# Block-sorted attention into a routed expert layer: values regrouped through DRAM, output turned by DMA transposes, and half-chunk first-layer blocks

## The chip, the cores and the metric

The kernel runs on one core of one Trainium2 chip. The metric is the device time of one execution in microseconds (us). Before the change it is 749.72 us, the median of 3 runs (749.62 to 749.95).

## The reference

Two stages follow each other. The first is an attention whose keys and values are sorted by blocks; the second a layer of eight experts that mixes all experts for each token.

```python
# q, k, v: batch 4, heads 8, seq 768, head_dim 64; sort_net: 4 x 8 x 8 x 8
P = sort_net
for _ in range(5):                       # Sinkhorn
    P = exp(P - max(P, -1)); P /= sum(P, -1); P /= sum(P, -2)
k_sorted = einsum('bhij,bhjcd->bhicd', P, k_blocks)     # 8 blocks of 96 rows
v_sorted = einsum('bhij,bhjcd->bhicd', P, v_blocks)
attn = softmax(q_block @ k_sorted_block.T / 8)          # within each block of 96
out  = attn @ v_sorted_block

x = out as 3072 tokens x 512             # (batch, seq) x (head, dim)
P = exp(x @ w_gate - max)                # 3072 x 8, then 8 Sinkhorn rounds
y = sum over e of P[:, e] * (relu(x @ w1[e]) @ w2[e])   # w1: 512x1024, w2: 1024x512
```

## The kernel before, in words

Matrix products are in bf16 with float32 sums. The attention works on 16 **pairs** of heads (pair m is heads 2m and 2m+1; four pairs make one batch). A token's row of 768 is split as 128 partitions x 6 (`p kk`), so that a block of 96 rows is 16 partitions x 6. `load_pair` (L83) loads k, v and q of one pair, 192 KB each in SBUF, with a cast from float32, from GpSimd's queue.

**Start.** `sort_net` is loaded, TensorE runs 24 filler matmuls on zeros (L116), and VectorE and ScalarE run the 5 Sinkhorn rounds (L121 to L135). `Prep` holds P widened to 1024 columns; eight matmuls (L140) make `Pbig`, from which `build_r` (L154) makes R of each pair, a 128x128 matrix per head that sorts blocks when it is multiplied.

**One pair passes through four stages**, each one iteration of the loop over m later than the one ahead of it:

- `stage1(m)` (L162): 12 matmuls for K and 12 for V (L171) give the sorted K and V with the head dimension on partitions, evicted as `KT` and `VT` (L176, L178); 12 transposes by TensorE (L182) and one copy (L185) give `QT`; then `build_r(m + 1)`.
- `stage2(m)` (L189): 16 matmuls for the scores (L197), four Exps (L200); 8 transposes by TensorE (L204) and a copy (L207) give `VS`, the sorted V with rows on partitions and a column of ones for the sum.
- `stage3(m)` (L209): 16 matmuls with V (L216), then four times a reciprocal and a scaling (L219, L220) into `OG`.
- `stage4(m)` (L223): 8 transposes by TensorE (L227) and one copy (L229) into `xtT`, the input of the second layer with features on partitions.

**Blocks between the stages.** Each iteration calls `fill(1)` four times (L268). It issues the next first-layer block `h_block` (L244): four matmuls of 512 columns (L249) for one expert e, one chunk c of 512 tokens and 128 of the 1024 hidden features, evicted with a ReLU by VectorE or ScalarE in turn (L253, L255). A chunk is free only when `state["done"]` has reached its last batch (`last_batch`); the list `early` gives the order. As long as no batch is done, `fill` issues one filler matmul (L266) in place of a block. `gate(b)` (L232) computes the logits of a batch. After the loop come 8 Sinkhorn rounds with three blocks in each (L312), and then the main part: second-layer tiles `y_tile` (L335: eight matmuls, L339, and one eviction with an add, L345) alternate with the remaining blocks. `HB` = 10 buffers hold first-layer chunks. The last expert's tiles are stored by SP (L349).

All engines run in the order in which the code issues (`tc.manual_schedule`). PSUM's eight banks are a pool that rotates. SP's queue has only the load of `sort_net` and the 24 stores; GpSimd's queue has all other loads (w1 at L95, w2 at L99). Tokens in `xtT` lie as `kk p`, so the stores at L349 write rows six apart.

Of the kernel before, what the change touches and what calls it, by code (L numbers as in the profile page):

```python
# [25 lines left out]
def kernel(  # L26
# [17 lines left out]
    HB = 10  # L44
    scale = 1.0 / (D ** 0.5)
# [6 lines left out]
    ps = ctx.enter_context(tc.tile_pool(name="ps", bufs=8, space=bass.MemoryType.PSUM))  # L52

    def bank(shape, dt=F32):
        return ps.tile(shape, dt, name="bank")
# [8 lines left out]

# [6 lines left out]
    mask = ones.tile([128, 16], F32)  # L71
    nc.vector.reduce_sum(out=mask, in_=ident.rearrange("p (j c) -> p c j", c=16), axis=AX.X)
# [6 lines left out]
    iop = actx.enter_context(tc.tile_pool(name="iop", bufs=5))  # L79
    atp_ = actx.enter_context(tc.tile_pool(name="atp", bufs=2))  # L80
    qkv = {}

    def load_pair(m):  # L83
        r = []
        for src, nm in ((kh, "kb"), (vh, "vb"), (qh, "qb")):
            t = iop.tile([128, 2, 6, 64], BF16, name=nm)
            nc.gpsimd.dma_start(out=t, in_=src[2 * m:2 * m + 2].rearrange("h p kk d -> p h kk d"))  # L87
            r.append(t)
        qkv[m] = r
# [11 lines left out]
    for m in range(4):  # L101
        load_pair(m)
# [3 lines left out]
    xtT = ones.tile([128, 4, B, 6, 128], BF16)  # L106
    xf = xtT.rearrange("d hp b kk p -> d hp (b kk p)")
# [6 lines left out]
    w_ = bank([128, 512])  # L114
    for _ in range(24):
        nc.tensor.matmul(w_, wide[:, 0:128], wide, start=True, stop=True)  # L116

    rs = ones.tile([32, 8], F32)
    Prep = ones.tile([32, 8, 8, 16], BF16)
    Pt = P.rearrange("p i j -> p j i")  # L120
    nc.vector.reduce_max(out=rs, in_=P, axis=AX.X)  # L121
    nc.vector.tensor_sub(P, P, mkap(rs, [rs.ap[0], rs.ap[1], [0, 8]]))
    for it in range(5):
        nc.scalar.activation(out=P, in_=P, func=AF.Exp)
        nc.vector.reduce_sum(out=rs, in_=P, axis=AX.X)
        nc.vector.reciprocal(out=rs, in_=rs)
        nc.vector.tensor_tensor(out=P, in0=P, in1=mkap(rs, [rs.ap[0], rs.ap[1], [0, 8]]),
                                op=ALU.mult)
        nc.vector.reduce_sum(out=rs, in_=Pt, axis=AX.X)
        nc.vector.reciprocal(out=rs, in_=rs)  # L130
        if it < 4:
            nc.vector.tensor_tensor(out=Pt, in0=Pt, in1=mkap(rs, [rs.ap[0], rs.ap[1], [0, 8]]),
                                    op=ALU.mult)
        else:
            nc.vector.tensor_tensor(out=Prep, in0=mkap(P, [P.ap[0], [8, 8], [1, 8], [0, 16]]),  # L135
                                    in1=mkap(rs, [rs.ap[0], [0, 8], [1, 8], [0, 16]]), op=ALU.mult)

    pbp = bank([128, 8, 32])
    for i in range(8):
        nc.tensor.matmul(pbp[:, i, :], Prep[:, i].rearrange("g j c -> g (j c)"),  # L140
                         ident[0:32, 0:32], start=True, stop=True)
    Pbig = ones.tile([128, 8, 32], F32)
    nc.vector.tensor_copy(Pbig, pbp)


    KT, VT, QT, ATT, VS, OG = {}, {}, {}, {}, {}, {}

    vs_ = [ones.tile([96, 8, 2, 65], BF16, name=f"vs{n}") for n in range(2)]
    for t in vs_:
        nc.vector.memset(t[:, :, :, 64:65], 1.0)  # L150

    Rt = {}

    def build_r(m):  # L154
        R = Rt[m] = atp_.tile([128, 2, 8, 16], BF16, name="R")
        nc.vector.tensor_tensor(
            out=R,
            in0=mkap(Pbig, [Pbig.ap[0], [1, 2], [32, 8], [0, 16]], off=2 * m),
            in1=mkap(mask, [mask.ap[0], [0, 2], [0, 8], [1, 16]]),
            op=ALU.mult)  # L160

    def stage1(m):  # L162
        kb, vb, qb = qkv[m]
        R = Rt[m]
        for src, dic, nm in ((kb, KT, "KT"), (vb, VT, "VT")):
            dic[m] = atp_.tile([128, 8, 6, 16], BF16, name=nm)
            for kh2 in range(2):
                b_ = bank([128, 3, 128])
                for k3 in range(3):
                    for h2 in range(2):  # L170
                        nc.tensor.matmul(b_[64 * h2:64 * h2 + 64, k3, :], src[:, h2, 3 * kh2 + k3, :],  # L171
                                         R[:, h2].rearrange("p i c -> p (i c)"), start=True, stop=True)
                dst = dic[m][:, :, 3 * kh2:3 * kh2 + 3, :].rearrange("d i kk c -> d kk i c")
                b_ = b_.rearrange("d kk (i c) -> d kk i c", c=16)
                if nm == "KT" or kh2 == 0:
                    nc.scalar.copy(dst, b_)  # L176
                else:
                    nc.vector.tensor_copy(dst, b_)  # L178
        b_ = bank([128, 6, 128], BF16)
        for kk in range(6):  # L180
            for h2 in range(2):
                nc.tensor.matmul(b_[64 * h2:64 * h2 + 64, kk, :], qb[:, h2, kk, :], ident,  # L182
                                 is_transpose=True, start=True, stop=True)
        QT[m] = atp_.tile([128, 6, 128], BF16, name="QT")
        nc.vector.tensor_copy(QT[m], b_)  # L185
        if m + 1 < NPAIR:
            build_r(m + 1)

    def stage2(m):  # L189
        ATT[m] = [atp_.tile([96, 2, 384], BF16, name=f"at{h2}") for h2 in range(2)]  # L190
        for half in range(2):
            bb = [bank([96, 4, 96]) for _ in range(2)]
            for i4 in range(4):
                i = half * 4 + i4
                for h2 in range(2):
                    hs = slice(64 * h2, 64 * h2 + 64)
                    nc.tensor.matmul(bb[h2][:, i4, :], KT[m][hs, i].rearrange("d kk c -> d (kk c)"),  # L197
                                     QT[m][hs, :, 16 * i:16 * i + 16], start=True, stop=True)
            for h2 in range(2):
                nc.scalar.activation(out=ATT[m][h2][:, half, :], in_=bb[h2].rearrange("k i q -> k (i q)"),  # L200
                                     func=AF.Exp, scale=scale)
        b_ = bank([96, 8, 128], BF16)
        for i in range(8):
            nc.tensor.matmul(b_[:, i, :], VT[m][:, i].rearrange("d kk c -> d (kk c)"), ident, is_transpose=True,  # L204
                             start=True, stop=True)
        VS[m] = vs_[m % 2]
        nc.vector.tensor_copy(VS[m][:, :, :, 0:64], b_.rearrange("c i (h d) -> c i h d", d=64))  # L207

    def stage3(m):  # L209
        OG[m] = atp_.tile([96, 8, 2, 64], BF16, name="OG")  # L210
        for half in range(2):
            for h2 in range(2):
                b_ = bank([96, 4, 65])
                for i4 in range(4):
                    i = half * 4 + i4
                    nc.tensor.matmul(b_[:, i4, :], ATT[m][h2][:, half, 96 * i4:96 * i4 + 96],  # L216
                                     VS[m][:, i, h2, :], start=True, stop=True)
                rc = atp_.tile([96, 4], F32, name="rc")
                nc.vector.reciprocal(out=rc, in_=b_[:, :, 64:65].rearrange("q i a -> q (i a)"))  # L219
                nc.vector.tensor_tensor(out=OG[m][:, 4 * half:4 * half + 4, h2, :], in0=b_[:, :, 0:64],  # L220
                                        in1=mkap(rc, [rc.ap[0], [1, 4], [0, 64]]), op=ALU.mult)

    def stage4(m):  # L223
        b, hpi = m // 4, m % 4
        b_ = bank([128, 8, 96], BF16)
        for i in range(8):
            nc.tensor.matmul(b_[:, i, :], OG[m][:, i].rearrange("q h d -> q (h d)"), ident[0:96, 0:96],  # L227
                             is_transpose=True, start=True, stop=True)
        nc.scalar.copy(xtT[:, hpi, b].rearrange("d kk (i c) -> d i kk c", c=16),  # L229
                       b_.rearrange("d i (kk c) -> d i kk c", c=16))  # L230

    def gate(b):  # L232
        b_ = bank([128, 6, E])
        for t in range(6):
            for kk in range(4):
                nc.tensor.matmul(b_[:, t, :], xtT[:, kk, b, t, :], wg[:, kk], start=(kk == 0),  # L236
                                 stop=(kk == 3))
# [3 lines left out]
    hT = {}  # L241
    flip = [0]

    def h_block(e, c, fb, both=False):  # L244
        if fb == 0:
            hT[e, c] = hp_.tile([128, 8, 512], BF16, name="hTs")
        b_ = bank([128, 512])
        for kk in range(4):
            nc.tensor.matmul(b_, w1t[e][:, kk, fb * 128:(fb + 1) * 128], xf[:, kk, c * 512:(c + 1) * 512],  # L249
                             start=(kk == 0), stop=(kk == 3))  # L250
        flip[0] ^= 1
        if both and flip[0]:
            nc.vector.tensor_scalar_max(hT[e, c][:, fb, :], b_, 0.0)  # L253
        else:
            nc.scalar.activation(out=hT[e, c][:, fb, :], in_=b_, func=AF.Relu)  # L255

    early = [(0, 0), (1, 0), (0, 1), (0, 2), (1, 1), (1, 2), (0, 3), (1, 3), (0, 4), (0, 5), (1, 4), (1, 5)]
    seq = early + [(e, c) for e in range(2, E) for c in range(6)]
# [147 lines left out]
```

The softmax here doesn't subtract the row's maximum and nothing guards it: scores larger than these inputs give would overflow.

## Time and profile before

| | us |
|---|---|
| median of 3 runs | 749.72 |
| the profiled execution | 750.19 |
| its span, first to last instruction | 748.4 |
| TensorE busy (matmuls / weight loads beside them) | 738.3 / 358.5 |
| ScalarE / VectorE / GpSimd busy | 274.2 / 252.1 / 48.9 |
| first-layer matmuls, L249 (1536) | 346.1 |
| second-layer matmuls, L339 (1536) | 338.0 |
| first sort (L171) starts at | 14.45 |
| iteration 7 starts at | 43.56 |
| first second-layer matmul at | 146.82 |

Times of day are us from the start of the span. "Busy" sums the instructions of an engine, with overlaps counted once. Matmuls are pipelined, so that the duration of one in the profile (379 ns for 512 columns) is more than its share of a row of them: in the chain of waits four take 0.86 us. The chain follows back from the last instruction, at each step to whatever ended the wait. The granted clock is the share of full speed that TensorE's throttle allowed. A DMA share over 1 means that transfers overlap within the engines.

### The profile page before, as it was taken

The page shows a single profiled execution, that of the slowest core. Times are in us where ns is not written, and L with a number is a line of the kernel's source. Part 1 is how long each engine was busy: PE and PEld are TensorE (multiplying, and loading weights), DVE is VectorE, ACT ScalarE, POOL GpSimd, SP SyncE. Part 2 cuts the span into 40 slices and gives each one's busy share as a digit, 9 for nine tenths or more (in the row PEclk, how much of TensorE's full clock was granted, in tenths as well). Part 3 has the DMA queues.
Part 4 walks back from the last instruction along what each step waited for, and adds up shares of the span by engine and source line. Part 5 has one row for each costly group of instructions (what it writes and reads, how often), then busy time and mean ns, then how long its engine had stood idle before and what let it go on. Part 6 is the DMA issues. An engine that isn't in the chain of part 4 may idle for free.

```text
span 748.4 us, 10663 instructions
## 1 busy us (share of the span) xinstructions
PE 738.3 (99%) x4588; PEld 358.5 (48%) x4588; DVE 252.1 (34%) x497; ACT 274.2 (37%) x497; POOL 48.9 (7%) x71
## 2 busy tenths in 40 slices
PE   6999999999999999999999999999999999999997
PEld 3776665444444444444444444444444444444443
DVE  5887775632122122122221221221221221212443
ACT  2776665513423423324324324234234233243000
POOL 8542000000000000000000000000000000000000
PEclk8999999999999999999999999999999999999999
DMA  9999100011300061200330032100330003000133
GB/s 149 204 205 163 19 2 1 1 20 38 56 1 1 0 96 29 46 1 1 56 57 1 0 57 40 19 0 1 57 56 1 1 0 57 1 0 1 43 154 141
DMA packets 29679, 33.21 MB, mean 44 GB/s; under 512 B 1984, under 2 KB 22464, under 8 KB 29632
## 3 DMA queue, kind: packets, MB, share of 16 engines
q0 software_dynamic: 26128, 26.23, 22.5%
q1 hardware_dynamic: 3504, 6.30, 2.2%
q8 instruction: 36, 0.59, 0.3%
q14 instruction: 11, 0.09, 0.0%
HBM read 52.45 MB, written 6.29 MB: 78 GB/s over the span
## 4 chain that ended last, share of the span: by engine, by line
PE 98%; DMA 1%; POOL 1%; DVE 0%; issue 0%; POOLq 0%
PE bank L249 44%; PE bank L339 44%; PE bank L171 2%; PE bank L216 2%; PE bank L204 1%; PE bank L197 1%; PE bank L266 1%; DMA qb<-in_q_dram 1%; PE bank L182 1%; PE bank L227 1%; PE bank L236 0%; POOL kb L87 0%; POOL vb L87 0%; PE bank L321 0%; POOL qb L87 0%; DVE osbl L345 0%
## 5 line engine op out<-in xcount | busy, mean ns | idle before, releaser
L255 ACT ACTIVATE hTs<-bank 128x512 bf16<-128x512 f32 x358 | 213.7, 597 | 371.2 <-PE bank L249 370.4
L249 PE MATMUL bank<-xtT,w1e 128*128 128x512 bf16 x1536 | 346.1, 379 | 0.0
L339 PE MATMUL bank<-w2e,hTs 128*128 128x512 bf16 x1536 | 338.0, 379 | 0.0
L345 DVE SCALAR_TENSOR_TENSOR osbl<-bank,glog,osbl 128x512 f32<-128x512 f32 x168 | 126.2, 751 | 398.7 <-PE bank L339 398.7
L339 PEld LDWEIGHTS <-hTs 128*128 128x128 bf16 x1536 | 150.2, 98 | 181.0
L249 PEld LDWEIGHTS <-w1e 128*128 128x128 bf16 x1536 | 147.9, 98 | 170.3
L342 DVE TENSOR_SCALAR osbl<-bank,glog 128x512 f32<-128x512 f32 x24 | 18.0, 751 | 54.7 <-PE bank L339 54.7
L220 DVE TENSOR_TENSOR OG<-bank,rc 96x256 bf16<-96x256 f32 x64 | 26.9, 421 | 2.2
L95 POOL DMA_DIRECT2D w1e<-in_moe_w_dram x8 | 6.0, 752 | 312.6 <-PE bank L249 312.3
L99 POOL DMA_DIRECT2D w2e<-in_moe_w_dram x8 | 7.1, 888 | 237.5 <-PE bank L339 237.1
L253 DVE TENSOR_SCALAR hTs<-bank 128x512 bf16<-128x512 f32 x26 | 17.7, 683 | 6.1 <-PE bank L249 6.1
L229 ACT COPY xtT<-bank 128x768 bf16<-128x768 bf16 x16 | 12.8, 798 | 14.1 <-PE bank L227 13.7
L176 ACT CAST KT<-bank 128x384 bf16<-128x384 f32 x32 | 13.8, 486 | 8.1 <-PE bank L171 7.9
L87 POOL DMA_DIRECT2D kb<-in_k_dram x16 | 11.5, 722 | 20.9 <-PE bank L171 20.1
L178 DVE CAST VT<-bank 128x384 bf16<-128x384 f32 x16 | 8.9, 553 | 11.2 <-PE bank L171 8.8
L219 DVE RECIPROCAL rc<-bank 96x4 f32<-96x4 f32 x64 | 10.9, 171 | 3.7 <-PE bank L216 3.7
L87 POOL DMA_DIRECT2D vb<-in_v_dram x16 | 11.5, 722 | 5.2 <-PE bank L266 2.5
L87 POOL DMA_DIRECT2D qb<-in_q_dram x16 | 11.6, 724 | 1.9 <-issue 0.3
L266 PE MATMUL bank<-wide 128*128 128x512 bf16 x28 | 10.6, 419 | 0.0
L204 PE MATMUL bank<-ident,VT 128*96 128x128 bf16 x128 | 10.4, 224 | 0.0
L171 PE MATMUL bank<-R,kb 128*64 128x128 bf16 x192 | 9.1, 234 | 1.0 <-DMA qb<-in_q_dram 1.0
L197 PEld LDWEIGHTS <-KT 64*96 64x96 bf16 x256 | 7.1, 121 | 5.8 <-issue 5.6
(152 smaller groups left out, 232.6 us busy)
## 6 DMA issues: line engine op xcount, KB each, us to landing
w1e<-in_moe_w_dram POOLq DMA_DIRECT2D x8, 1024.0 KB, 8.1
w2e<-in_moe_w_dram POOLq DMA_DIRECT2D x8, 1024.0 KB, 8.9
out_dram<-osbl SPq DMA_DIRECT2D x24, 256.0 KB, 2.0
kb<-in_k_dram POOLq DMA_DIRECT2D x16, 192.0 KB, 7.3
vb<-in_v_dram POOLq DMA_DIRECT2D x16, 192.0 KB, 7.3
qb<-in_q_dram POOLq DMA_DIRECT2D x16, 192.0 KB, 7.3
P<-in_sort_net_dram SPq DMA_DIRECT2D x1, 8.0 KB, 1.7
wg<-in_moe_w_gate_dram POOLq DMA_DIRECT2D x1, 8.0 KB, 6.8
```

What stands on the lines that cost most here:

```text
L87: nc.gpsimd.dma_start(out=t, in_=src[2 * m:2 * m + 2].rearrange("h p kk d -> p h kk d"))
L171: nc.tensor.matmul(b_[64 * h2:64 * h2 + 64, k3, :], src[:, h2, 3 * kh2 + k3, :], R[:, h2].rearrange("p i c -> p (i c)"), start=True, stop= ...
L204: nc.tensor.matmul(b_[:, i, :], VT[m][:, i].rearrange("d kk c -> d (kk c)"), ident, is_transpose=True, start=True, stop=True)
L216: nc.tensor.matmul(b_[:, i4, :], ATT[m][h2][:, half, 96 * i4:96 * i4 + 96], VS[m][:, i, h2, :], start=True, stop=True)
L220: nc.vector.tensor_tensor(out=OG[m][:, 4 * half:4 * half + 4, h2, :], in0=b_[:, :, 0:64], in1=mkap(rc, [rc.ap[0], [1, 4], [0, 64]]), op=AL ...
L249: nc.tensor.matmul(b_, w1t[e][:, kk, fb * 128:(fb + 1) * 128], xf[:, kk, c * 512:(c + 1) * 512], start=(kk == 0), stop=(kk == 3))
L253: nc.vector.tensor_scalar_max(hT[e, c][:, fb, :], b_, 0.0)
L255: nc.scalar.activation(out=hT[e, c][:, fb, :], in_=b_, func=AF.Relu)
L266: nc.tensor.matmul(b_, wide[:, 0:128], wide, start=True, stop=True)
L339: nc.tensor.matmul(b_, hT[e, c][:, fb, tt * 128:(tt + 1) * 128], w2t[e][:, fb, :], start=(fb == 0), stop=(fb == 7))
L342: nc.vector.tensor_scalar(out=osbl[:, t, :], in0=b_, scalar1=glog[:, t, e:e + 1], scalar2=None, op0=ALU.mult)
L345: nc.vector.scalar_tensor_tensor(out=osbl[:, t, :], in0=b_, scalar=glog[:, t, e:e + 1], in1=osbl[:, t, :], op0=ALU.mult, op1=ALU.add)
```

## The change

1. **Values of pairs 4 to 15** (`m >= MB`, 4). V is sorted as rows, two matmuls of 384 columns with R as weights; the result VR goes to DRAM (`vd`) and comes back regrouped into `VS` (`v_back`), by two DMAs on SP. The 8 transposes and the copy of stage 2 are left out for them.
2. **Output of pairs 4 to 15.** `OG` goes to DRAM (`xd`) and is turned into `xtT` by one DMA transpose on SP (`x_back`), issued at the next iteration's start. Stage 4 is left out for them. Batches count as done in iterations 6, 11, 15 and 19 instead of 6, 10, 14 and 18 (the first one fill earlier than before), and gates move.
3. **Half blocks.** A block can cover 256 tokens instead of 512; it is free when the batch of its own last token is done. The order `early` changes: chunks 1 of both experts and chunk 4 of expert 0 are cut into halves.
4. **Start.** Q is loaded first; Q of pairs 0 to 2 is turned during the Sinkhorn rounds, with ScalarE copying; 6 filler matmuls in each round; P is transposed as 64 columns and widened by a constant matrix `sel` (made by ScalarE); R of pair 0 is made straight from PSUM.
5. **Order of tokens.** `KT`, `QT`, `VT` and `xtT` lie in natural order; the evictions of K, V and Q write with a step of six elements, and the output rows are stored next to each other.
6. **Smaller ones.** PSUM is one tile with a hand-turned bank number; stage 3 takes one reciprocal and one scaling per head over two banks; loads run five pairs ahead instead of four, w1 of expert 1 is asked for in iteration 4, w2 in 13 and 15; the last tile is done in two halves.

```diff
+    QA = 3
+    MB = 4
+    SP_ = 1
+    SQ_ = 6
+    AH = 5
+    W1B = 4
+    FILL = [(1, 1, 1, 1)] * 18 + [(1, 1, 1, 2), (1, 1, 2, 2)]
...
-    for m in range(4):
-        load_pair(m)
+    for src, m in ((qh, 0), (qh, 1), (kh, 0), (vh, 0), (qh, 2), (kh, 1), (vh, 1), (kh, 2), (vh, 2),
+                   (qh, 3), (kh, 3), (vh, 3)) + tuple((s_, m) for m in range(4, AH) for s_ in (kh, vh, qh)):
+        load(src, m)
...
+    sel = ones.tile([64, 64, 16], BF16)
+    nc.scalar.copy(sel, mkap(ident, [[ident.ap[0][0], 64], [1, 64], [0, 16]]))
...
         nc.scalar.activation(out=P, in_=P, func=AF.Exp)
+        if 1 <= it <= QA:
+            q_turn(it - 1, "act")
+        spin(SQ_)
...
+    b_ = bank()[0:64, 0:32]
+    nc.tensor.matmul(b_, Pb, ident[0:32, 0:32], start=True, stop=True)
+    PT = ones.tile([64, 32], BF16)
+    nc.vector.tensor_copy(PT, b_)
...
+    build_r(0, pbp)
+    nc.vector.tensor_copy(Pbig, pbp)
...
+            VR = atp_.tile([128, 6, 2, 64], BF16, name="VR")
+            t = qkv[id(vh), m]
+            for h2 in range(2):
+                b_ = bank()[:, 0:384]
+                nc.tensor.matmul(b_, Rt[m][:, h2].rearrange("p i c -> p (i c)"),
+                                 t[:, h2].rearrange("p kk d -> p (kk d)"), start=True, stop=True)
...
+            vd[m] = drp.tile([128, 768], BF16, name="vd")
+            nc.sync.dma_start(out=vd[m], in_=VR.rearrange("p kk h d -> p (kk h d)"))
+        if m >= QA:
+            q_turn(m, "dve")
...
+        for h2 in range(2):
+            b_ = bank2()[0:96, :, 0:260].rearrange("q f (i e) -> q f i e", i=4)
...
+            nc.vector.reciprocal(out=rc, in_=b_[:, :, :, 64 * h2])
...
+        if m >= MB:
+            xd[m] = drp.tile([768, 128], BF16, name="xd")
+            nc.sync.dma_start(out=xd[m].rearrange("(i q) e -> q i e", i=8),
+                              in_=OG[m].rearrange("q i h d -> q i (h d)"))
+
+    def v_back(m):
+        if m >= MB:
+            VS[m] = vs_[m % 3]
+            nc.sync.dma_start(out=VS[m][:, :, 1:129],
+                              in_=vd[m].rearrange("(i c) (kk e) -> (c kk) i e", c=16, kk=6))
+
+    def x_back(m):
+        if m >= MB:
+            nc.sync.dma_start_transpose(out=xtT[:, m % 4, m // 4, :], in_=xd[m])
...
+    early = [(0, 0, 0, 512), (1, 0, 0, 512), (0, 1, 0, 256), (1, 1, 0, 256), (0, 1, 256, 512), (1, 1, 256, 512),
+             (0, 2, 0, 512), (1, 2, 0, 512), (0, 3, 0, 512), (1, 3, 0, 512), (0, 4, 0, 256), (0, 4, 256, 512),
+             (0, 5, 0, 512), (1, 4, 0, 512), (1, 5, 0, 512)]
...
+        if 3 <= m <= NPAIR + 2:
+            x_back(m - 3)
+        fill(f[0], spins=SP_)
         if 1 <= m <= NPAIR:
             stage2(m - 1)
-        fill(1)
+        if m < NPAIR:
+            v_back(m)
+        fill(f[1], spins=SP_)
...
+        if m in (6, 11, 15, 19):
+            state["done"] += 1
+        fill(f[3], spins=SP_)
+        if m in (8, 12, 16, 19):
+            gate({8: 0, 12: 1, 16: 2, 19: 3}[m])
```

## The prediction

> **What bounds the kernel now.** I read the page's busy row first, then its slices, then the chain of work that ended last in order of time, and last the stages in windows. The busy row, the clock and the DMA share of the page:
>
> ```profile
> PE 738.3 (99%) x4588; PEld 358.5 (48%) x4588; DVE 252.1 (34%) x497; ACT 274.2 (37%) x497; POOL 48.9 (7%) x71
> ...
> PEclk8999999999999999999999999999999999999999
> DMA  9999100011300061200330032100330003000133
> ```
>
> TensorE is never without work except in the first 18.7 us slice, where also its clock is down. The two big matmul groups are 3072 matmuls of 512 columns at 0.216 us (four take 0.86 us in the chain), 663 us, and the change leaves them as they are. What can move is the other 85 us: the wait before the first sort, the cold clock, and the small attention matmuls. Chain of waits, one start and one steady iteration (start us, us, what):
>
> ```profile
> 14.46 1.48 PE bank L171 x24
> 15.94 0.64 PE bank L182 x12
> 16.58 1.82 PE bank L266 x4
> ...
> 50.96 0.79 PE bank L171 x24
> 51.75 0.34 PE bank L182 x12
> 52.09 0.97 PE bank L249 x4
> 53.06 0.49 PE bank L197 x16
> 53.55 0.58 PE bank L204 x8
> 54.12 0.86 PE bank L249 x4
> 54.99 0.71 PE bank L216 x16
> 55.69 0.86 PE bank L249 x4
> 56.56 0.34 PE bank L227 x8
> 56.90 0.86 PE bank L249 x4
> ```
>
> An iteration takes 6.8 us with no gap, so a small matmul removed here is removed from the end. The same 24 sorting matmuls cost 1.48 us at 14.46 and 0.79 us later. Windows tell why (PE, PEld, DVE, ACT, POOL busy, granted clock, DMA share, GB/s):
>
> ```profile
> 9.00:13.00 4.00, 0.34 (x2) 0.00 (x0) 3.40 (x12) 0.26 (x1) 3.00 (x5) 1.00 1.30 198
> ...
> 14.00:16.00 2.00, 1.55 (x31) 1.55 (x31) 0.41 (x4) 0.98 (x3) 1.26 (x3) 0.50 1.31 201
> ...
> 18.00:20.00 2.00, 2.00 (x33) 1.67 (x34) 0.14 (x1) 1.10 (x3) 1.17 (x2) 0.50 1.29 205
> ...
> 25.00:30.00 5.00, 5.00 (x100) 3.89 (x99) 4.75 (x15) 3.81 (x10) 2.72 (x4) 1.00 1.31 202
> ```
>
> TensorE idles from 9.3 to 13.1 us, and the clock is then 0.50 until about 20.4. Note also the last columns: the DMA engines are full at some 200 GB/s written throughout this stage.
>
> **The change, part by part.** The sum is made against the profiled execution's own 750.19 us (span 748.4 and 1.8 around it); the median of the runs shown is 0.47 us below, which I take off at the end.
>
> *The start.* The first sort waits for R at 14.39, the end of the Sinkhorn chain. Its tail gets shorter: the 1.21 us Prep row becomes a 0.26 us one; a transposing matmul and a 0.2 us copy come in; R is made from the bank directly (0.42) with Pbig's 0.42 us copy behind it. That is 1.05 us less. But ScalarE gets four new copies. The sel copy (64x1024) takes about 1.0 us by the 0.80 us row of 768 elements and ends at 3.5 where the first Exp stood ready at 2.9: +0.6. The three Q copies (0.8 each) stand between the Exps of a 1.81 us round. The first two fit almost (+0.1). The third needs the fifth load, which by the trace's landing records arrives at 10.54 (first at 4.92, second at 7.57, then one per 0.98 us), so the last Exp goes from 10.9 to 11.9: +1.0. Sum: first sort at 14.95, **+0.5**. Bounds: -1.0 if the copies fit, +1.5 if scattered writes make them 1.2 us each.
>
> *The clock.* Six idle-time matmuls per round and the Q transposes fill the hole at 9.3 to 13.1 but for some 1.1 us (the wait for the fifth load). The stretch 14.46 to 20.46, 6.0 us at half clock, then takes 3.0: **-3.0**. Transposes of Q for three pairs leave the path, 3 x 0.34: **-1.0**. One filler matmul becomes a first-layer block moved earlier: **-0.2**. New waits: R of pair 1 behind Pbig (0.15), the block right behind stage 4 of pair 3, which needs its 0.80 us copy (0.3): **+0.45**.
>
> *Pairs 4 to 15.* The transposes of V go (0.58 x 12 = **-7.0**, two of them before pair 7), those of the output too (0.35 x 12 = **-4.2**). V's sort becomes two matmuls of 384 columns; at 0.216 per 512 they take 0.33 instead of 0.40, and one more change of array tiling comes in, which the row of 0.97 against 0.86 puts at 0.11: **0**, bounds -0.8 and +1.3. Iterations fall from 6.8 to 5.9. Scores read Q in one run instead of six; 16 take 0.49 and two at a time would stream in 0.32: bounds -2.7 and 0, I take 0.
>
> *Half blocks.* 48 half blocks instead of 24, 96 more matmuls. From nothing to 3.6 us (192 x 0.019, what the eight 128-column matmuls of L204 take beyond their stream); weights load beside the stream, so the near end: **+0.3**.
>
> *Evictions.* In an iteration of before (64.57 to 71.37) VectorE is busy 5.37 and ScalarE 4.69. VectorE loses the V copy (0.69) and 0.45 of the reciprocals and scalings, now two pairs on 512 elements instead of four on 256; ScalarE loses the 0.80 xtT copy. Q's copy now writes every sixth element. No row shows such a write; the nearest are
>
> ```profile
> L185 DVE COPY QT<-bank 128x768 bf16<-128x768 bf16 x16 | 8.8, 548 | 0.2
> L318 DVE TENSOR_REDUCE cs_2838<-glog 128x8 f32<-128x192 f32 x8 | 4.0, 501 | 0.3
> L314 DVE TENSOR_REDUCE rs_2837<-glog 128x24 f32<-128x192 f32 x8 | 2.8, 353 | 0.4
> ```
>
> The reduction that strides takes 0.77 ns per element more than the one that doesn't, so the copy lies between 0.55 and 1.54 us; I take 0.95, one element per cycle of the 0.68 us row for 512. With half blocks (0.42 and 0.38 us by the slope between 384 and 512) VectorE then needs 4.9 to 5.5 and ScalarE 4.3 to 4.9 of 5.9 us. Both fit, VectorE tightly; before, it was at 4.04 of 4.40 (30.7 to 35.1) with TensorE still unbroken. I take **+0.7** for banks freed late; bounds 0 and 5. On this the Trainium skill speaks against the change: SBUF — State Buffer, Door 1, says a line holds 16 bytes and that fewer than two hits per line cost bandwidth; a 12-byte step is such a pattern. By it the sum would sit at the dear end; the strided reduction (32-byte step) agrees, and no row here shows a 12-byte write.
>
> *The new transfers.* Per pair SP issues vd, v_back, xd and x_back, 192 KB each. Latency is covered: a store to DRAM lands 2.0 us after issue (out_dram), v_back has about two iterations until stage 3, x_back eleven first-layer blocks before the last gate. On SP only these wait behind one another. What they cost is room: a load takes 0.98 us (about 400 GB/s read), three per pair plus 5.5 us for a w1. Without new traffic w1 of expert 1 would land at 46.2; its first use, the fourth block of iteration 8, comes at 50.9 in my sum. By then 12 new copies and two transposes are queued. At 0.5 us each (half a load's bytes) that is 7.0 us, 2.3 late; if they slip between the loads, 0. I take **+1.2**. If the cover is gone TensorE simply stands. Afterwards a pair asks 2.9 + 2.0 us of the DMA engines against 5.9 of TensorE, which fits. The transpose's own time has no row: no less than the 0.5 of a copy, and as far as 12 us (768 rows of 256 bytes one by one at the 16 ns of the sort_net packets); I take the near end, as it moves the bytes of a copy. The Trainium skill (DMA: Bandwidth & Descriptors, Latency and other measured facts) gives 261 GB/s for a DMA transpose; an estimate from it is 0.75 us, which would put 0.5 us more on the late weight and nothing else.
>
> *The end.* The last tile is evicted in halves: the last 0.75 becomes 0.42: **-0.35**.
>
> Sum: 0.5 - 3.0 - 1.0 - 0.2 + 0.45 - 7.0 - 4.2 + 0.3 + 0.7 + 1.2 - 0.35 = -12.6. 750.19 - 12.6 = 737.6, and 737.1 on the scale of the runs. I call it 737.
>
> **Rivals.**
> 1. *The DMA engines become the bound; slower.* With T us per transpose, w1 is late by 1.3 + 2T, and pairs 10 to 15 each lose T - 1.46 (2.94 of loads + 1.5 of copies + T against 5.9). At T = 4 that is 24.5 us: 761. It turns the gain into a loss from T = 2.65 on. For it: the share of 1.31 while loads run. Against: loads end by about 64 us in before, and bytes alone give T = 0.5.
> 2. *VectorE or ScalarE becomes the bound.* Q's copy at 1.54 and K's casts likewise scattered: VectorE at 5.5 of 5.9, queueing costs 0.4 to 0.5 in each of nine iterations: 741. For it: the strided reduction. Against: 92% busy before without a gap.
> 3. *The clock is not held.* The change's fillers leave a hole at the fifth load and while Pb, PT and R are made; if that is enough, or a wait for w1 cools TensorE, the 3.0 us come back: 740.5. Against: 1.1 us of hole where before had 3.8.
> 4. *All covers hold.* No late weight, no late banks, quicker scores: 732 to 734.
>
> **How the numbers follow.** Forecast 737 (734 to 740): 0.42. Rival 4: 0.15. Rival 2: 0.13. Rival 3: 0.13. Rival 1: 0.13 slower, and 0.04 where it eats the gain within 0.2%, about what a measurement of this kernel can tell from no change. So faster 0.83, same 0.04, slower 0.13. The range leaves out those 0.17 and a little below: 730 to 748.
>
> **What would show it.** Right: the first sort at about 15 us at full clock, L204's and L227's successors only for four pairs, iterations of 5.9 us, x_back landing in 2 to 3 us, and at most one gap in TensorE near 51 us. Wrong: TensorE waiting on a DMA in each iteration (rival 1), on VectorE or ScalarE banks (2), a clock of 0.50 after 14 us (3). I would be wrong most of all if one transpose kept the DMA engines for several us.

## The result, and the profile after

The changed kernel takes **781.35 us** (median of 4 runs, 780.03 to 782.0) against 749.67 us before: a ratio of 1.042, 95% interval [1.0402, 1.0438]. The profiled execution took 782.0, its span is 780.2. The prediction, 737 in a range of 730 to 748, had the sign wrong.

The same rows of the page as before the change, of the changed kernel:

```profile
PE 744.2 (95%) x4318; PEld 365.2 (47%) x4390; DVE 268.4 (34%) x428; ACT 305.3 (39%) x503; POOL 49.2 (6%) x74
...
PEclk9689889999999999999999999999999999999999
DMA  9999986403030005220033003300330000200033
```

TensorE has 36 us without work where it had 10 (99% busy became 95%), and the clock is down in four of the first six slices. The whole loss lies in the attention part: the first second-layer matmul comes at 182.66 instead of 146.82. Chain of waits, start and one steady iteration (start us, us, what; pieces of under 0.05 us left out):

```profile
11.91 2.63 ACT QT L147
...
17.74 0.55 PE PS L213 x6
18.31 2.72 ACT KT L218 x2
21.03 1.28 ACT VT L218
...
50.76 0.34 PE PS L232
51.12 0.56 DVE VR L238
51.68 2.63 DVE QT L149
54.35 0.69 PE PS L272 x12
```

Before, the chain held matmuls only in these iterations. Now it runs through the copies of Q and the casts of K and V. Groups of instructions, shapes kept apart (xcount | busy us, mean ns | idle before):

```profile
L218 ACT CAST KT<-PS 128x384 bf16<-128x384 f32 x32 | 43.9, 1560 | 9.8 <-PE PS L213 9.4
L149 DVE COPY QT<-PS 128x768 bf16<-128x768 bf16 x13 | 35.4, 2725 | 0.6 <-issue 0.3 <-PE PS L142 0.2
L147 ACT COPY QT<-PS 128x768 bf16<-128x768 bf16 x3 | 8.0, 2796 | 1.0 <-PE PS L142 1.0
L220 DVE CAST VT<-PS 128x384 bf16<-128x384 f32 x4 | 5.8, 1442 | 7.3 <-PE PS L213 7.3
```

The copy of Q was 548 ns in the group shown before the change; K's cast was 486. Both engines now need 3.5 to 4.1 ns per element written with a step of 12 bytes (2725 / 768, 1560 / 384).

From iteration 1 on an iteration takes 6 to 9 us, and one, iteration 10, takes 17.28 (84.88 to 102.16). Windows there (PE, PEld, DVE, ACT, POOL busy, granted clock, DMA share, GB/s), TensorE's longest wait (us in total, times, longest), and SP's queue (issue at, us to issue):

```profile
80.00:85.00 5.00, 4.50 (x50) 2.48 (x50) 4.66 (x7) 4.04 (x8) 2.72 (x4) 1.00 1.40 127
85.00:90.00 5.00, 3.79 (x49) 1.88 (x48) 4.57 (x5) 4.67 (x8) 0.00 (x0) 1.00 1.36 71
90.00:95.00 5.00, 0.00 (x0) 0.00 (x0) 0.26 (x1) 0.38 (x2) 0.00 (x0) 0.67 1.22 174
95.00:100.00 5.00, 2.50 (x19) 1.75 (x20) 0.20 (x1) 0.00 (x0) 0.00 (x0) 0.50 1.22 195
```

```profile
PE PS L272 <- DMA vs_265<-vd: 8.0, 1, 8.0
```

```profile
80.33 1.18 SPq L292 DMA_TRANSPOSE xtT<-xd  x1
81.62 0.52 SPq L287 DMA_DIRECT2D vs_265<-vd  x1
82.19 1.95 SPq L281 DMA_DIRECT2D xd<-OG  x1
84.23 7.84 SPq L240 DMA_DIRECT2D vd<-VR  x1
102.71 1.14 SPq L292 DMA_TRANSPOSE xtT<-xd  x1
```

TensorE stands still from 89.46 to 97.50 for the return of V, asked for at 81.62 (landed 15.84 us later), and its clock drops to 0.50. By the transfer records, the transpose of 80.33 landed after 11.34 us (median of the twelve: 3.1), the store of 82.19 after 20.46. That store holds up the same iteration a second time. It is the piece of the chain of waits that spans it:

```profile
82.19 20.46 DMA xd<-OG
```

`OG` has two buffers, so VectorE waits for this store before it can write the next output (4.1 us, until 102.74), and the sort of iteration 11 waits 0.97 us behind VectorE. At 80.91 and 81.80, in iteration 9, GpSimd had issued the two loads of w2 that are written for iterations 13 and 15: its queue holds no other work after the last pair's loads, so nothing makes it wait. The w2 loads run from 86 to 105. In each 2 us of 92 to 96 the records show 305 packets of 1024 bytes (w2) and 305 or 306 of 256 bytes (SP): one for one.

### The profile page after: what moved, and what is told of

It reads as the page before. It is cut to its first block, busy times and chain, and to the rows that moved or that the text cites. A ratio compares the mean times of both kernels' runs of the same rounds, so it can differ in the third digit from the quotient of the medians.

```text
span 780.2 us, 10299 instructions
## 1 busy us (share of the span) xinstructions
PE 744.2 (95%) x4318; PEld 365.2 (47%) x4390; DVE 268.4 (34%) x428; ACT 305.3 (39%) x503; POOL 49.2 (6%) x74
## 4 chain that ended last, share of the span: by engine, by line
PE 87%; ACT 4%; DVE 4%; DMA 3%; issue 1%; ACTq 0%; DVEq 0%
PE PS L421 42%; PE PS L321 40%; DMA xd<-OG 3%; DVE QT L149 2%; ACT KT L218 2%; PE PS L272 1%; PE PS L133 1%; ACT QT L147 1%; PE PS L213 1%; ACT VT L218 1%; PE PS L232 0%; DVE VR L238 0%; PE PS L308 0%; DVE OG L276 0%; PE PS L254 0%
## 5 line engine op out<-in xcount | busy, mean ns | idle before, releaser
L327 ACT ACTIVATE hTs<-PS 128x512 bf16<-128x512 f32 (+1 forms) x372 | 215.2, 579 | 396.6 <-PE PS L321 381.6
L321 PE MATMUL PS<-xtT,w1e 128*128 128x512 bf16 (+1 forms) x1597 | 344.6, 368 | 3.2 <-DVE QT L149 1.0
L421 PE MATMUL PS<-w2e,hTs 128*128 128x512 bf16 (+1 forms) x1513 | 335.9, 378 | 1.6
L427 DVE SCALAR_TENSOR_TENSOR osbl<-PS,glog,osbl 128x512 f32<-128x512 f32 (+1 forms) x169 | 126.4, 748 | 398.3 <-PE PS L421 375.6
L218 ACT CAST KT<-PS 128x384 bf16<-128x384 f32 x32 | 43.9, 1560 | 9.8 <-PE PS L213 9.4
L424 DVE TENSOR_SCALAR osbl<-PS,glog 128x512 f32<-128x512 f32 x24 | 18.0, 751 | 51.2 <-PE PS L421 50.2
L149 DVE COPY QT<-PS 128x768 bf16<-128x768 bf16 x13 | 35.4, 2725 | 0.6 <-issue 0.3
L276 DVE TENSOR_TENSOR OG<-PS,rc 96x512 bf16<-96x512 f32 x32 | 22.0, 687 | 5.1 <-DMA xd<-OG 4.1
L325 DVE TENSOR_SCALAR hTs<-PS 128x512 bf16<-128x512 f32 (+1 forms) x36 | 19.8, 567 | 11.2 <-PE PS L321 9.2
L133 PE MATMUL PS<-wide 128*128 128x512 bf16 x55 | 19.9, 478 | 2.4 <-DVE wide L84 1.2
L254 PE MATMUL PS<-QT,KT 64*96 64x96 bf16 x256 | 12.7, 224 | 8.1 <-ACT KT L218 6.2
```

What stands on the lines that cost most here:

```text
L133: nc.tensor.matmul(b_, wide[:, 0:128], wide, start=True, stop=True)
L254: nc.tensor.matmul(bb[h2][:, 96 * i4:96 * i4 + 96], KT[m][hs, i].rearrange("d c kk -> d (c kk)"), QT[m][hs, 16 * i:16 * i + 16].rearrange( ...
L276: nc.vector.tensor_tensor(out=OG[m][:, :, h2, :].rearrange("q (f i) d -> q f i d", f=2), in0=b_[:, :, :, 1 - h2:65 - h2], in1=mkap(rc, [rc ...
L325: nc.vector.tensor_scalar_max(hT[e, c][:, fb, lo:hi], b_, 0.0)
L327: nc.scalar.activation(out=hT[e, c][:, fb, lo:hi], in_=b_, func=AF.Relu)
L421: nc.tensor.matmul(b_, hT[e, c][:, fb, tt * 128:(tt + 1) * 128], w2t[e][:, fb, ns], start=(fb == 0), stop=(fb == 7))
```

## The experiments

Two theories stood against each other after the result. **A**: the evictions that write with a step of six elements bind ScalarE and VectorE. **B**: SP's transfers are late, because the DMA engines give them one small packet for each packet of a load. Both hold, in different iterations; a third theory, that the way through DRAM itself costs more than the transposes, fell with run 11. An eviction writes "in one run" when it writes element after element, without a step. Where an experiment writes Q, K and V so without moving the rows back, its rows are in another order and so is its output; the instructions are as many.

**1. Evictions in one run.**

```diff
-        dst = QT[m].rearrange("d p kk -> d kk p")
+        dst = QT[m].rearrange("d p kk -> d (p kk)").rearrange("d (kk p) -> d kk p", kk=6)
```

(K and V alike.)

> The evictions of Q, K and V write their 384 or 768 elements in one run instead of with a step of six, so rows land in a wrong order; everything else stays. Theory A (the scattered writes, 2.7 us for a Q copy and 1.56 us for a K cast, hold up the stages, and the two w2 loads in iteration 10 cost another 11 us): first sort near 15 us, Q copy near 0.55 and K cast near 0.5 us, iterations of 5.9 to 6.3 us, the long iteration stays; 745 to 756 us. Rival B (the way through DRAM holds up every iteration): over 772 us.

Measured: 765.04 us, ratio 1.0204 [1.0187, 1.0221]. Groups of this run:

```profile
L217 ACT CAST KT<-PS 128x384 bf16<-128x384 f32 x32 | 13.8, 484 | 10.6 <-PE PS L213 10.2
L149 DVE COPY QT<-PS 128x768 bf16<-128x768 bf16 x13 | 7.1, 549 | 0.3 <-ACT VR L235 0.3
```

The two durations are back, and 16.3 us with them, but two iterations are slow: 16.9 us from 10 to 11, as in the change, and 13.9 from 6 to 7, which took 7.5 in the change. In that one TensorE waits 7.2 us for the first return of V, a wait that the change does not have; so 16.3 us is a net figure. The time lies between the two expectations, and the first sort still comes at 17.64, not near 15: there is more than one cause.

**2. w2 after the last gate.** A copy of the last gate's logits on GpSimd stands ahead of the two loads.

```diff
-        if m == 13:
-            load_w2(0)
-        if m == 15:
-            load_w2(1)
...
+    hold = ones.tile([128, 1], F32)
+    nc.gpsimd.tensor_copy(hold, glog[:, NT - 1, 0:1])
+    load_w2(0)
+    load_w2(1)
```

> The two loads of w2 before the main part are held back by a small GpSimd copy that waits for the last gate; everything else stays. Theory A: iteration 10, 17.3 us long, falls to about 7.5, the rest stays: 781.4 - 10 = 771 us (767 to 775). Rival C (the transposes and the stores behind them stall on SP's queue by themselves): a stall of over 8 us stays somewhere in iterations 8 to 12, 778 to 783 us.

Measured: 769.28, 1.0268 [1.025, 1.0287]: A. Iteration 10 fell from 17.28 to 7.00 us; no wait of TensorE on a return of V is left in the list of waits, and the store of the output is gone from the chain. So w2 costs the change 12.1 us.

**3. Both.**

> Both edits: evictions of Q, K and V in one run (rows in a wrong order) and the w2 loads held back. Theory A: the two causes together are the whole of the miss, so what the prediction had for the rest comes out: 737 us (734 to 743), TensorE without a gap of over 1 us after 20 us. Rival B or C: over 760 us.

Measured: 754.29, 1.0065 [1.005, 1.008]. The two causes add up (16.3 + 12.1 = 28.4; 27.1 measured), but 754 was expected by neither theory: a third cause is left. It is the step from iteration 6 to 7, 14.72 us. Windows and the longest wait of this run:

```profile
40.00:45.00 5.00, 0.38 (x5) 0.08 (x1) 0.18 (x1) 1.59 (x4) 2.35 (x4) 0.85 1.16 207
45.00:50.00 5.00, 1.64 (x17) 1.44 (x18) 0.72 (x2) 0.00 (x0) 0.71 (x1) 0.50 1.22 215
```

```profile
PE PS L271 <- DMA vs<-vd: 9.5, 3, 8.0
```

The picture is that of w2, one load earlier: the first return of V, issued at 36.24, lands at 48.31, while w1 of expert 1 is loaded (to 48.64). From 42 to 44 there are 173 packets of 2048 bytes (172 ns each) and 177 of 256.

**4. Nothing through DRAM, evictions as in the change** (`MB = 16`).

> All 16 pairs take the way over TensorE (V transposed and the output turned by TensorE), as the first four do; scattered writes, start and order of blocks stay. Theory A: no way through DRAM, so the 11 us of iteration 10 go, and TensorE's 11 us of transposes come back; the scattered writes stay, V's cast now scattered too on both engines (1.4 to 1.7 us each): 778 to 792 us. Rival B: the DRAM way was the cost, so 745 to 762 us.

Measured: 797.53, 1.0643 [1.0621, 1.0665]: slower still, above A's range too and far from B's, so leaving the way through DRAM out does not win the time back. But the run also brings 12 pairs of V's casts with a step (1659 and 1441 ns), and the waits on `KT` and `VT` grow; so it cannot price the way through DRAM. Run 11 does.

**5. Without the load of w1 of expert 1**, on top of run 3.

```diff
         if m == W1B:
-            load_w1(1)
+            w1t[1] = w1t[0]
```

> Evictions in one run and w2 late, as in the run of 754.3 us, and the load of expert 1's first-layer weights left out (expert 1 multiplies with expert 0's weights, so the output is another). Theory A: the third cause is that the first return of V (issued 36.2, landed 48.3) shares the DMA engines packet for packet with that load's 2048-byte packets; without it the step from iteration 6 to 7 falls from 14.7 to 4-7 us, total 742-747. Rival B: the return of V is late beside any load (8.2 us was seen beside 768-byte packets), so it still lands at about 44.5 where stage 3 wants it at 40.4: iteration 6 to 7 takes 8-9 us, total 748-752.

Measured: 750.72, 1.0025 [1.0014, 1.0036]: rival B. Without that load TensorE still waits 5.1 us for the first return of V; the k, v and q loads hold it up as well. So the third cause is not one load but the time at which the traffic on SP begins.

**6. DRAM from pair 6 on**, with the load (`MB = 6`, on top of run 3).

> The same with the load kept, but V and output go through DRAM only from pair 6 on (two pairs more by TensorE, 2 x 0.93 us more work by the rows of before). Theory A: traffic on SP's queue now begins at about 40 us, the return of pair 6 at 45, when the load of expert 1's weights is nearly done: 754.3 - 10.5 - 1 + 1.9 = 744.7, range 743-748, no wait of TensorE above 3 us on a DMA. Rival B: the return is late beside the k, v and q loads too and the wait comes again two iterations later: 752-757.

Measured: 746.32, 0.9972 [0.996, 0.9983]: A. The longest wait for a return is 2.3 us, though two more pairs are done by TensorE.

**7. and 8. The token order of before.** If only the step costs, the output can stay the reference's: with keys lying as `kk c` and x as `kk c i`, no eviction needs a step in its write. For that V's rows come out of the sort as `c i`, so R is built as `c i`, and the sort of K reads it with a step.

```diff
-        R = Rt[m] = atp_.tile([128, 2, 8, 16], BF16, name="R")
+        R = Rt[m] = atp_.tile([128, 2, 16, 8], BF16, name="R")
...
-                                     Rt[m][:, h2].rearrange("p i c -> p (i c)"), start=True, stop=True)
+                                     Rt[m][:, h2].rearrange("p c i -> p i c"), start=True, stop=True)
```

> The change with the token order of before: keys lie as kk c and x as kk c i, so that Q, K and V are evicted in one run and the output is still the reference's (R is built as c i, the sort of K reads it with a step of 8; rows of 256 bytes in the store of V and in its return, rows of 2048 bytes in the store of the attention output). Theory A: only the scattered writes made the evictions dear, so this is worth as much as the run with rows in wrong order: 762-768, copies of Q near 550 ns and casts of K near 500 ns. Rival B: what the order of before costs elsewhere (Q read in six runs, R with a step, V's store in 768 rows) takes part of it back: 769-776.

Measured: 776.84, 1.0372 [1.0355, 1.0389], just above rival B's range. Run 8 is the same with w2 late and `MB = 6`.

> The token order of before, w2 asked for after the last gate, DRAM from pair 6 on. Theory A (three causes: scattered writes, w2, w1 of expert 1): 743-749, below the kernel before. Rival B: V's 768 rows in both directions on SP's queue are late beside the loads: 751-758.

Measured: 765.24, 1.022 [1.0205, 1.0235], 7 us above rival B's. Both miss on the side of rival B, and beyond it. The group of K's sort, in run 7 and in the last run (14), where R is read in one run again:

```profile
L213 PE MATMUL PS<-R,kb 128*64 128x128 bf16 x192 | 24.7, 405 | 0.9 <-DMA kb<-in_k_dram 0.5 <-DMA vb<-in_v_dram 0.3
```

```profile
L221 PE MATMUL PS<-R,kb 128*64 128x128 bf16 x192 | 8.4, 223 | 0.6 <-DVE R L191 0.5
```

The evictions were as expected (549 and 479 ns), but my repair put a step into an operand of TensorE: 16.3 us more busy time, on the engine that sets the end.

**9. and 10. R kept twice**, `i c` for K and `c i` for V (one more build on VectorE), w2 late, from pair 6 and from pair 8 on.

> As the run of 765.2 us (token order of before, w2 late, DRAM from pair 6 on), but R is kept twice: as i c for the sort of K, read in one run, and as c i for the weights of V's sort (one more build of 0.58 us on VectorE per pair). Theory A: the 19 us between that run and the 746.3 us of the one with rows in wrong order are the sort of K, whose moving operand was read with a step of 16 bytes (405 ns per matmul against 223): 745-749, K's sort back at about 223 ns. Rival B: the order costs elsewhere (V's rows, Q in six runs): 753-766.

Measured: 750.29, 1.0013 [1.0004, 1.0021]. K's sort is back at 223 ns and 15 us are won, but the time lies between the two ranges: iteration 8 takes 13.75 us. Its chain holds `vd<-VR` (issued 40.15, landed 49.51) and then `vs<-vd` (49.58 to 58.20): in this order the store of V has 768 rows of 256 bytes where run 6 had 128 rows of 1536 (landed after 5.87), and beside the loads it is late as well.

> The same with DRAM from pair 8 on, when all but the last loads have landed. Theory A (V's return waits only beside loads): two pairs more by TensorE cost 1.9, the 2.3 us wait and about 2 us of slow iterations go: 744-748. Rival B: the transfers are late among themselves: 748-752.

Measured: 745.48, 0.9944 [0.9932, 0.9957]. With the loads nearly over, TensorE waits for no return of V: A, and 0.56% faster than the kernel before.

**11. Nothing through DRAM, evictions without a step** (`MB = 16`, token order of before, w2 late).

> Nothing through DRAM: token order of before, all pairs by TensorE, the rest of the change kept (start, half blocks, two-bank stage 3), w2 late. Theory A: the way through DRAM gives 0.93 us for a pair when it is covered, so against the run of 746.3 us this costs 10 x 0.93 and saves the 4-5 us of waits left in that one: 750-753. Rival B: the way through DRAM gives little even where it is covered: 743-748.

Measured: 749.55, 1.0002 [0.9993, 1.0011]: between A and B. This is the price list that the prediction lacked. One iteration by TensorE (run 11) and one through DRAM (run 14), from their chains:

```profile
73.53 0.79 PE PS L213 x24
74.32 0.34 PE PS L142 x12
74.65 0.98 PE PS L322 x8
75.63 0.49 PE PS L254 x16
76.12 0.58 PE PS L262 x8
76.70 0.87 PE PS L322 x8
77.57 0.71 PE PS L272 x16
78.28 0.87 PE PS L322 x8
79.15 0.34 PE PS L300 x8
79.50 0.87 PE PS L322 x8
```

```profile
83.15 0.46 PE PS L221 x12
83.60 0.43 PE PS L240 x2
84.03 0.46 PE PS L142 x12
84.49 0.98 PE PS L331 x8
85.47 0.49 PE PS L264 x16
85.96 0.98 PE PS L331 x8
86.94 0.71 PE PS L282 x16
87.64 1.75 PE PS L331 x16
```

6.84 us against 6.24. The transposes are worth 0.92 (0.58 + 0.34) as forecast, but the sorts with Q go from 1.13 to 1.35 and the block behind the scores from 0.87 to 0.98. So a pair through DRAM is worth 0.6 us when nothing is late. Runs 11 and 10 give a little less: (749.55 - 745.48) / 8 = 0.51.

**12. Q's copy reads with a step instead of writing with one**, the change otherwise untouched.

```diff
-        dst = QT[m].rearrange("d p kk -> d kk p")
+        dst = QT[m]
+        b_ = b_.rearrange("d kk p -> d p kk")
```

> The change as it is, but the copy of Q writes in one run and reads PSUM with a step (128 rows of 6, 256 bytes apart); casts of K and V still write with a step. Theory A: only a write with a step is dear: the copy falls from 2725 to 550-800 ns, about half of the 16 us of the scattered writes goes: 770-776. Rival B: a read with a step is as dear: copy above 2 us, 778-784.

Measured: 775.2, 1.0344 [1.032, 1.0369]: A, with 6.2 of the 16.3 us won.

```profile
L150 DVE COPY QT<-PS 128x768 bf16<-128x768 bf16 x13 | 12.5, 958 | 0.6 <-ACT KT L219 0.3 <-PE PS L142 0.2
L148 ACT COPY QT<-PS 128x768 bf16<-128x768 bf16 x3 | 2.4, 798 | 3.7 <-PE PS L142 3.7
```

The same permutation costs 0.96 us on VectorE (0.55 without any step, 2.73 with the step in the write), and nothing on ScalarE.

**13. and 14. The start.** Run 11 left open why the start gives nothing. Run 13 turns Q of two pairs only in the Sinkhorn rounds (`QA = 2`); run 14 loads Q of the third pair third.

```diff
-    for src, m in ((qh, 0), (qh, 1), (kh, 0), (vh, 0), (qh, 2), (kh, 1), (vh, 1), (kh, 2), (vh, 2),
+    for src, m in ((qh, 0), (qh, 1), (qh, 2), (kh, 0), (vh, 0), (kh, 1), (vh, 1), (kh, 2), (vh, 2),
```

> The run of 745.5 us with Q of only two pairs turned in the Sinkhorn rounds. Theory A: the last Exp goes back to about 10.7, the first sort to 14.0-14.3, and 0.34 us of transposes come back in iteration 2: 743.8-744.8. Rival B: without the third pair's transposes TensorE has a longer hole and its clock goes to half in the first iterations: 745.5-748.

> The run of 745.5 us with all three early loads of Q ahead of the first K and V. Theory A: the first sort comes at 15.97 instead of the forecast 14.95 because the third copy of Q waits for its load (landed 11.24) and holds the last Exp (12.55, against 10.7 by the rounds of 1.81); with the load third it lands by 8 and the first sort comes at 14.2-14.5: 743.5-744.5. Rival B: the sort then waits for K and V, or the end is set by later loads: no change, 745-746.

Measured: 744.5, 0.9942 [0.9928, 0.9956], and 743.97, **0.9936 [0.9924, 0.9949]**, the fastest kernel of this study; both as A expected. ScalarE's timeline, run 10 and then run 14:

```profile
11.85 0.80 ACT L147 COPY QT<-PS 128x768 bf16<-128x768 bf16 x1 [2.69 <-PE PS L142]
12.55 0.25 ACT L164 ACTIVATE P<-P 32x64 f32<-32x64 f32 x1
```

```profile
9.74 0.80 ACT L147 COPY QT<-PS 128x768 bf16<-128x768 bf16 x1 [0.58 <-PE PS L142]
10.72 0.26 ACT L164 ACTIVATE P<-P 32x64 f32<-32x64 f32 x1 [0.18 <-DVE P L174]
```

The last Exp stood behind a copy that waited for a load. With the load moved, the first sort comes at 14.15 instead of 15.97, and the clock stays at 1.00 (windows from 8 to 20 us of run 14).

## Why the prediction was wrong, point by point

Forecast 737.1 and measured 781.35 are 44.3 us apart. Two steps failed outright, one term had the wrong size, and the gain at the start did not last.

- **Evictions: failed.** "I take 0.95" for Q's copy, between bounds of 0.55 and 1.54 (0.95 and 768 times the reduction's 0.77 ns), and K's casts not at all (only rival 2 had them). Measured 2.73 and 1.56. The near rows were reductions that *read* with a step; run 12 shows that a read with a step is cheap where a write with one is dear. So the upper bound was no bound: no row of before told of such a write. Forecast +0.7, measured +16.3 net (run 1). Rival 2 named the mechanism with a price of 4 us. The rule weighed there, the Trainium skill's SBUF — State Buffer, Door 1 (full bandwidth needs two hits in a 16-byte line), pointed the right way; it gives no time for it, the trace does. The same remark counts 8 bf16 elements as a distance that costs nothing; here a step of 6 in the write costs 2725 ns against 549, and the measurement decides.
- **The new transfers: failed.** "Latency is covered: a store to DRAM lands 2.0 us after issue". That row is of stores of 2 KB rows that run alone. V's return and the store of the output have rows of 256 bytes. Beside a load they landed after 5 to 20 us; even with the loads over, v_back takes 3.7 to 5.2 and a transpose 2.6 to 4.8 (run 14, from 66 us on). Forecast +1.2; measured 12.1 for w2 (run 2), which I had not seen coming forward, though the trace of before shows both early loads of w2 issued ahead of the iteration that asks for them (48.51 against 50.89, 67.91 against 71.30). About 11 more are the first returns, as an estimate: run 3's 754.29 against 749.55 - 12 x 0.55 = 743. In the change itself this part is covered: there the evictions make V's first return so late (52.35) that expert 1's w1 has landed (49.27), it takes 6.55 us, and TensorE does not wait for it. What was charged as room on the engines (0.5 us per copy) was a turn in a queue: a transfer of 48 small packets per engine waits out 48 packets of the load. At 172 + 31 ns each that gives 9.7 us, as an estimate; 12.07 were measured with another store in the same queue. The Trainium skill, DMA: Bandwidth & Descriptors, Queues, rings and completion order, says that each engine turns round between queues packet by packet. The records agree, with 305 to 305; the 9 to 17 descriptors that the page puts into a typical packet are not seen in them.
- **V and output transposes, -7.0 and -4.2: mechanism right, size off.** They went, but the term for V's sort and one more change of tiling, taken as 0 with an upper bound of 1.3 in all, is 0.33 us per pair (0.22 in the sorts with Q, 0.11 in the block behind the scores); whether it is the tiling that lengthens them was not tested. Worth 6 to 7 us in 12 pairs (12 x 0.51 to 0.60, an estimate), not 11.2. A steady iteration takes 6.25, not 5.9.
- **Start +0.5, clock -3.0, Q -1.0, filler -0.2, waits +0.45: not got.** In the change the first sort came at 17.74 (forecast 14.95), behind three copies of Q in a row, and the clock was at half from 16.6 to 30.2: rival 3's condition. The copies are not its only cause. Without the step the first sort came at 15.97 in run 10, because Q's third load landed at 11.24, not 10.54; and in the profiled executions of runs 1 and 11, where TensorE waited for the same load, the clock was at half from 12.7 to 16.1 and from 11.2 to 14.6, and the first sort came at 17.64 and 17.42. In run 14 the gain is there at first and does not last: iteration 3 starts at 22.70 against 26.33 before, 3.6 us ahead, but iteration 8 at 49.17 against 50.89, 1.7 ahead and not 3.2. Iterations 3 to 5 take 4.6 to 4.9 us where before they took 4.2 to 4.4, and iteration 6, which holds the block that moved forward, 5.6. The chain of run 14 passes there through Exps and the scalings of stage 3:

```profile
27.42 0.70 DVE OG L286
...
34.56 1.25 ACT at L268 x3
```

In the chain of before these iterations are matmuls only. Which of the edits does it, the hand-turned banks or the scalings over two banks, no run tells.
- **Half blocks +0.3: right.** Eight half-width matmuls take 0.87, four full ones 0.86.
- **End -0.35: about right.** The last eviction is 0.48 instead of 0.75 and its store lands in 1.72 instead of 2.00. (The reading ahead of it, that TensorE is without work in the first slice only, passed over this end: the last digit of the page's PE row before is a 7.)
- **Rival 1** (the DMA engines become the bound) had the right side, and its deciding point, a transpose of more than 2.65 us, lies below the 3.1 that a transpose took to land (how long it kept the engines busy wasn't separated). Its mechanism did not decide, though: transposes of 2.6 to 4.8 us in run 14 hold nobody up, as x_back has time. What decided was the return of V and the store of the output beside loads. Its counter-argument was misread, too: loads do not end by about 64 us in before, the last q lands at 71.26 and the second w2 at 77.65.

Put together: evictions and w2 27.1 (run 3) and returns 11.3 instead of 0.7 + 1.2, that is 36.5 more; V's sort 4.6 (11.2 - 12 x 0.55); the start 3.1 (run 11's 749.55 against 746.4, the forecast without V, output, evictions and transfers). The sum is the 44.3 but for rounding, as it must be: each term is the difference of two runs or of a run and the forecast, so the sum is an account and no check of its own. The shares depend on the order, too: the wait for the first returns shows only once the evictions are fast.

The change does not lose because of its idea. Without the steps, with R kept twice, w2 held back, Q loaded first and DRAM from pair 8 on, it gains 5.2 us (749.21 to 743.97).

## What to carry to other kernels

In this kernel a permutation was cheapest in the read of an eviction (958 ns against 549 on VectorE, nothing more on ScalarE); in a write of two-byte elements with a step it cost up to five times the copy, and in TensorE's moving operand 405 ns against 223. A transfer of small rows beside a load of large ones is to be priced by its packets times the load's packet and its own (9.7 us estimated, 12.07 measured), and whoever writes a load for a later iteration must check that something makes its queue wait until then. A bound taken from the nearest row holds only if that row does the same thing on the same side (read or write, alone or beside other traffic).

## What the runs showed of the hardware that was not expected

- Writing bf16 with a step of 12 bytes takes 2725 ns for 768 elements on VectorE and 2796 on ScalarE, against 549 and 798 without a step. Reading PSUM with a step of 256 bytes costs 958 and 798.
- A matmul of 128 columns whose moving operand is read with a step of 16 bytes takes 405 ns instead of 223.
- Packets of two queues come in equal numbers, whatever their size: 256-byte packets of 31 ns against 1024-byte ones of 96 ns (305 to 305 in 2 us) and 2048-byte ones of 172 ns (177 to 173). A transfer of 192 KB in 256-byte rows landed after 2.3 to 5.2 us with the loads over (run 14), 5 to 9 beside 768-byte packets (the change, runs 3 and 6), 12 beside w1 (run 3) and 16 to 20 beside w2 (the change).
- Issuing can block: the store of V at 84.23 kept SP's queue for 7.84 us, with three transfers ahead of it not yet landed.
